# A decode step of attention plus a gated MLP on one core: whole wo loads, w_out on 128 lanes, another order of the last tiles, and part of wq's last rows on 2, 4 and 8 transfer engines

## The chip, the core and the metric

The kernel runs on one core of a Trainium2 chip. The core has TensorE (PE, matrix products, with its weight loads listed apart as PEld), VectorE (DVE), ScalarE (ACT), GpSimd (POOL) and SyncE (SP), which here issues nearly all transfers. Sixteen transfer engines (numbered 0 to 15 below) move data from the chip's memory (HBM) to the on-chip memory of 128 partitions, also called lanes. PE writes its results to an accumulator memory of its own (PSUM). The engines run on their own queues and wait for one another through semaphores.

The metric is the device time of one execution in microseconds (us): the median of several runs.

## The reference

Four sequences (B = 4), one new token each, model width D = 640. Both branches read the layer-normalised x.

- Attention: q = xn @ wq gives 32 heads of 128. Each of the 128 pairs of sequence and head has its own cache of 4096 keys and 4096 values of 128. The scores are q.k / sqrt(128); softmax over 4096; the weighted sum of the values; then all heads @ wo (4096 x 640).
- Gated MLP: z = gelu(xn @ w_in), 1728 wide, cut into z1 and z2 (Fh = 864 each); z2 is layer-normalised, multiplied by the scalar w_sp and shifted by b_sp (the sequence length is one); z1 times this @ w_out (864 x 640).

```python
xn = _layernorm(x, axis=-1)
return x + _A_ref(xn, k_cache, v_cache, wq, wo) + _B_ref(xn, w_in, w_sp, b_sp, w_out)
```

All data is bf16. The caches are 2 x 134 MB; the other inputs together are below 14 MB.

## The kernel before

**Tiles.** The caches are cut into NT = 32 tiles each of keys and of values: tile i holds 4 heads (HT) of one sequence. A tile is 128 partitions x 16384 elements, 4 MB, and one load (L118) brings it; partition p has 128 positions (NC) of one head. Tiles of four sequences form a group; there are HG = 8 groups.

**Slots.** Key and value tiles, the two parts of wq, and w_in with w_out share five slots (`KV_SLOTS`). A load can be issued when what was in its slot before has been used. The list `loads` (L123) is the order in which tiles are loaded: k0, k1, then v and k in turn, then k30, k31 and the last four values. `load_to(n)` issues loads up to the n-th of this list and is called at fixed places of the main loop. The last value tile comes in four pieces (`V_CUTS`).

**Per key tile**, in four quarters: `product` (DVE, L370) multiplies keys by the query, `fold_half` (DVE, L382) adds the two halves of each key, `sums` (PE, L394) adds further with an identity as weights, `row_sums` (DVE, L405) finishes the scores. `lane_max`, `turn_max`, `head_max`, `spread_max` and `exps` make the softmax weights of a tile during the next one. `weighted` (PE, L462) multiplies a value tile by its weights, 128 small matmuls. After four tiles of a group `group_den`, `group_norm` and `group_proj` divide and multiply by that group's wo rows (L492).

**Order.** The instructions of PE, DVE, ACT and SP stand in each queue as the program writes them (`manual_schedule`, L509). In the main loop tile i's keys are used, and the values of tile `lag`: i - 1 up to 28, none at 29, i - 2 after that. Tile 30's values come after the loop, between the softmax steps of tile 31, and then tile 31's in four cuts.

**Loads of weights.** SP issues, in this order: wq's first four rows of each partition (L90, 4 MB), its fifth rows (1 MB, 8 KB in each partition), w_in (L101), w_out (L102), k0, k1. wq, x and w_in are laid out so that partition p holds rows 5p to 5p + 4; the normalised x is turned to the same layout by five transposes (L197). w_out lies on 96 partitions of nine rows (FP = 96, NFC = 9), so w_in's columns are read with a step of nine (L248) and the MLP's hidden values are on 96 partitions. wo comes by group (`load_wo`, L137), one load of 128 partitions x 4 x 640 in one buffer; group 5's alone is cut into loads of 8, 4, 2, 1, 1 and 112 partitions (`WO_PROBE`), and the last group's into four, by head.

**The DMA semaphores.** Loads take eight semaphores in turn; a load whose semaphore still belongs to an earlier one is issued only after that one has landed. A load is divided over several transfer engines, and each of these adds one event to its semaphore.

Of the kernel before, what the change touches and what calls it, by code (L numbers as in the profile page):

```python
# [13 lines left out]
AX = mybir.AxisListType  # L14

KV_SLOTS = 5
PROBED = 5
WO_PROBE = (0, 8, 12, 14, 15, 16, 128)


@with_exitstack
def kernel(
# [34 lines left out]
    HD2 = Dh // 2  # L57
    RW = 8
    SLOT = NC * Dh
    FP = 96  # L60
    NFC = Fh // FP
    NOH = D // 2
    assert NFC * FP == Fh
# [14 lines left out]
    def slot(name):  # L78
        return kv.tile([P, SLOT], BF16, tag="kv", name=name)
# [5 lines left out]

    wq_v = A_wq.rearrange("(p c) n -> p c n", c=DC)
    wq_parts = []
    for c0, c1 in ((0, HT), (HT, DC)):
        t = slot("wq")[:, 0 : (c1 - c0) * HD].rearrange("p (c n) -> p c n", n=HD)
        nc.sync.dma_start(out=t, in_=wq_v[:, c0:c1, :])  # L90
        wq_parts += [(t, i) for i in range(c1 - c0)]

    wsp_bf = const.tile([1, 1], BF16)
    bsp_bf = const.tile([1, 1], BF16)
# [2 lines left out]

    w_sb = slot("w_sb")
    w_in_sb = w_sb[:, 0 : DC * F].rearrange("p (c n) -> p c n", c=DC)
    w_out_sb = w_sb[0:FP, DC * F : DC * F + NFC * D].rearrange("p (k n) -> p k n", k=NFC)  # L100
    nc.sync.dma_start(out=w_in_sb, in_=B_w_in.rearrange("(p c) n -> p c n", c=DC))  # L101
    nc.sync.dma_start(out=w_out_sb, in_=B_w_out.rearrange("(p k) n -> p k n", k=NFC))  # L102

    def kv_view(cache, i):
        hg, b = divmod(i, Bsz)
# [15 lines left out]
        tiles[i] = t[:].rearrange("p (c d) -> p c d", d=Dh)  # L121

    loads = [("k", 0), ("k", 1)]  # L123
    for i in range(NT - 4):
        loads += [("v", i), ("k", i + 2)]
    loads += [("k", NT - 2), ("k", NT - 1)] + [("v", i) for i in range(NT - 4, NT)]
    n_loaded = [0]

    def load_to(n):
        while n_loaded[0] < min(n, len(loads)):  # L130
            load(*loads[n_loaded[0]])
            n_loaded[0] += 1

# [3 lines left out]
    def load_wo(j):  # L137
        wo_tiles[j] = wop.tile([P, HT, D], BF16, name="wo")
        if j == HG - 1:
            for hh in range(HT):  # L140
                nc.sync.dma_start(out=wo_tiles[j][:, hh, :], in_=wo_v[j][:, hh, :])
            return
        cuts = WO_PROBE if j == PROBED else (0, P)
        for p0, p1 in zip(cuts, cuts[1:]):
            nc.sync.dma_start(out=wo_tiles[j][p0:p1], in_=wo_v[j][p0:p1])

    load_to(2)

# [43 lines left out]
    )  # L192

    xn_v = xn_bf[:].rearrange("b (p c) -> b c p", c=DC)
    xnT_ps = ps_m.tile([P, DC, Bsz], BF16, tag="m")
    for c in range(DC):
        nc.tensor.transpose(  # L197
            out=xnT_ps[:, c, :], in_=xn_v[:, c, :], identity=ident[:Bsz, :Bsz]
        )
    xnT = const.tile([P, DC, Bsz], BF16)  # L200
# [34 lines left out]

    gm = {}
    for name in ("zz", "gw", "gt", "gz"):
        gm[name] = work.tile([FP, 2, NFC, Bsz], FP32, name=name)
    gm["sq"] = work.tile([FP, NFC, Bsz], FP32, name="sq")
    gm["st"] = work.tile([1, 5 * Bsz], FP32, name="st")  # L240
    gm["ac"] = work.tile([1, 2 * Bsz], FP32, name="ac")
    gm["yT"] = work.tile([FP, NFC, Bsz], BF16, name="yT")

    def gmlp():
        zz, gw, gt, gz, sq = (gm[n] for n in ("zz", "gw", "gt", "gz", "sq"))
        zT = ps_pv.tile([FP, 2, NFC, Bsz], FP32, tag="pv", name="zT")
        for t in range(2):
            w_t = w_in_sb[:, :, t * Fh : (t + 1) * Fh].rearrange("p c (f k) -> p c k f", k=NFC)  # L248
# [25 lines left out]
        for src, at in ((gz[:, 1, :, :], 0), (sq[:], Bsz)):  # L274
            for k in range(NFC):
                nc.tensor.matmul(  # L276
                    out=s_ps[:, at : at + Bsz],
                    lhsT=ones_sq[:FP, 0:1],
                    rhs=src[:, k, :],
                    start=(k == 0),  # L280
                    stop=(k == NFC - 1),
                )
# [41 lines left out]
        nc.vector.tensor_tensor(  # L324
            out=sq[:],
            in0=gz[:, 1, :, :],
            in1=ac_sb[:FP, None, 0:Bsz].to_broadcast([FP, NFC, Bsz]),
            op=ALU.mult,
        )
        nc.vector.tensor_tensor(  # L330
            out=sq[:],
            in0=sq[:],
            in1=ac_sb[:FP, None, Bsz : 2 * Bsz].to_broadcast([FP, NFC, Bsz]),
            op=ALU.add,
        )
        nc.vector.tensor_tensor(out=gm["yT"][:], in0=gz[:, 0, :, :], in1=sq[:], op=ALU.mult)
        for k in range(NFC):
            for half in range(2):
                nc.tensor.matmul(
                    out=out_sum(half),  # L340
                    lhsT=gm["yT"][:, k, :],
                    rhs=w_out_sb[:, k, half * NOH : (half + 1) * NOH],
                    start=False,
                    stop=False,
                )
# [56 lines left out]
    def row_sums(i, half):  # L402
        if half == 0:
            scores[i] = small.tile([P, NC], FP32, name="s_sb")
        nc.vector.tensor_reduce(  # L405
            out=scores[i][:, half * HC : (half + 1) * HC],
            in_=sums_ps.pop((i, half))[:],
            axis=AX.X,
            op=ALU.add,
        )  # L410

    def lane_max(i):
        m1 = small.tile([P, 1], FP32, name="m1")
        nc.vector.tensor_reduce(out=m1[:], in_=scores[i][:], axis=AX.X, op=ALU.max)  # L414
        maxes[i] = m1
# [84 lines left out]
    def group(i, fn):  # L500
        if 0 <= i < NT and i % Bsz == Bsz - 1:
            fn(i // Bsz)

    def at(i, fn, *args):
        if 0 <= i < NT:
            fn(i, *args)

    E = mybir.EngineType
    with tc.manual_schedule(engines={E.PE, E.DVE, E.Activation, E.SP}):  # L509
        stage_q(0)  # L510
        stage_q(1)
        gmlp()
        load_to(3)
        for i in range(NT):
            lag = i - 1 if i < NT - 3 else None if i == NT - 3 else i - 2
# [5 lines left out]
            if i < NT - 1:  # L521
                group(i - 2, group_proj)
# [81 lines left out]
```

## Time and profile before

| | |
|---|---|
| time, median of 3 runs | 681.03 us (680.99 to 681.11) |
| the profiled execution's own time | 680.97 us |
| its span | 679.2 us |
| PE, DVE, ACT busy | 406.8, 506.7, 94.3 us |
| bytes from HBM | 282.24 MB, 416 GB/s over the span |
| products L370 | 128 x 2286 ns |
| folds L382 | 128 x 1219 ns |
| zT matmuls L251 | 90, 15.6 us together |
| waits of DVE's products for key tiles | 81.9 us |

The page cuts the span into 40 slices; its rows are busy tenths, and under DMA the mean share of the 16 transfer engines with the GB/s that they moved. The chain of waits goes back from the last instruction to what released it, again and again. The transfer view can be asked for one stretch of time: packets, MB, and the share of 16 engines that the packets' durations make up. The trace also holds each packet (size, start, duration) and each semaphore event of a load; it does not name the engine of a packet, but packets of one engine follow each other without a gap, so an engine can be followed.

### The profile page before, as it was taken

Reading aid. Unit: us, or ns where it says so; the run is one execution under the profiler, and the core shown is the slowest. Engines: PE = TensorE matmul, PEld = TensorE weight load, DVE = VectorE, ACT = ScalarE, POOL = GpSimd, SP = SyncE. Lnnn points to the kernel's source line nnn. Section 1 sums busy time; section 2 is a strip of 40 time slices with the busy share of each in tenths; the row PEclk is TensorE's granted clock in tenths of the full one; section 3 lists DMA queues with packets and bytes.
Section 4 is the critical chain, followed back from the end, with each engine's and each line's share of the span. In section 5 each row is a group of like instructions: output and inputs, shape, how many; then the busy total and the mean of one; then the engine's idle time right before and its main releaser. Section 6 shows DMA issues by size and latency. Waiting matters only on the chain.

```text
span 679.2 us, 11555 instructions
## 1 busy us (share of the span) xinstructions
PE 406.8 (60%) x5225; PEld 227.8 (34%) x5225; DVE 506.7 (75%) x432; ACT 94.3 (14%) x329; POOL 2.7 (0%) x12
## 2 busy tenths in 40 slices
PE   1945777556656556665555665555664456655677
PEld 1931334323332233333223333223333133331345
DVE  1069999877779777688776778687766877779991
ACT  0111211101111100111110111110111101111111
POOL 1000000000000000000000000000000000000000
PEclk9999675567656656656566756555665667656665
DMA  9999999999999999999999999999999999999994
GB/s 374 375 432 432 427 431 422 427 432 430 421 432 428 431 430 423 429 431 432 429 422 429 431 429 426 427 428 431 429 349 405 429 430 429 424 428 431 430 419 168
DMA packets 14563, 282.99 MB, mean 417 GB/s; under 512 B 1350, under 2 KB 5458, under 8 KB 5714
## 3 DMA queue, kind: packets, MB, share of 16 engines
q1 hardware_dynamic: 14494, 282.25, 98.3%
q8 instruction: 41, 0.67, 0.4%
q14 instruction: 8, 0.07, 0.0%
q10 hardware_dynamic: 20, 0.01, 0.0%
HBM read 282.24 MB, written 0.01 MB: 416 GB/s over the span
## 4 chain that ended last, share of the span: by engine, by line
DMA 63%; DVE 18%; PE 17%; issue 1%; ACT 0%; SPq 0%; DVEq 0%
DMA k_nat<-in_A_k_cache_dram 55%; DVE prod L370 10%; PE s_ps L394 8%; DMA v_nat<-in_A_v_cache_dram 5%; PE pv L462 5%; DVE folded L382 5%; DMA w_sb<-in_B_w_in_dram 3%; PE zT L251 2%; DVE s_sb L405 2%; DVE m L414 1%; ACT pm L447 0%; DVE nm L424 0%; PE qbc_ps L356 0%; PE out_ps L492 0%; PE ln_ps L276 0%
## 5 line engine op out<-in xcount | busy, mean ns | idle before, releaser
L370 DVE TENSOR_TENSOR prod<-k_nat,qbc 128x4096 bf16<-128x4096 bf16 x128 | 292.6, 2286 | 83.5 <-DMA k_nat<-in_A_k_cache_dram 81.9
L394 PE MATMUL s_ps<-folded,ident 128*128 128x512 bf16 x512 | 225.6, 621 | 74.5 <-DVE folded L382 74.5
L382 DVE TENSOR_TENSOR folded<-prod 128x2048 bf16<-128x2048 bf16 x128 | 156.1, 1219 | 3.3
L394 PEld LDWEIGHTS <-ident 128*128 128x128 bf16 x512 | 71.9, 141 | 182.9 <-issue 182.0
L462 PE MATMUL pv<-pm,v_nat 128*128 128x4 bf16 x4096 | 111.7, 167 | 2.2 <-DMA v_nat<-in_A_v_cache_dram 1.8
L462 PEld LDWEIGHTS <-v_nat 128*128 128x128 bf16 x4096 | 109.3, 100 | 7.4 <-DMA v_nat<-in_A_v_cache_dram 2.9
L419 PE MATMUL mT<-ident_f,m 128*1 128x128 f32 x32 | 11.2, 351 | 114.4 <-DVE m L414 114.4
L447 ACT ACTIVATE pm<-s_sb,nb 32x128 bf16<-32x128 f32 x128 | 73.9, 577 | 2.6
L443 ACT COPY nb<-nb_ps 128x4 f32<-128x4 f32 x32 | 5.2, 162 | 477.9 <-PE nb_ps L435 477.9
L435 PE MATMUL nb_ps<-nm,scale_row 1*128 1x4 f32 x64 | 18.0, 349 | 57.9 <-DVE nm L424 57.9
L419 PEld LDWEIGHTS mT<-ident_f,m 128*1 128x1 f32 x32 | 2.5, 79 | 140.9 <-DVE m L414 112.1
L405 DVE TENSOR_REDUCE s_sb<-s_ps 128x64 f32<-128x512 f32 x64 | 43.6, 681 | 7.3 <-PE s_ps L394 4.3
L435 PEld LDWEIGHTS nb_ps<-nm,scale_row 1*128 1x128 f32 x64 | 15.9, 305 | 67.5 <-issue 56.7
L447 ACT ACTIVATION_READ_ACCUMULATOR pm<-s_sb,nb 32x1 f32 x128 | 32.1, 251 | 0.0
L478 DVE RECIPROCAL rden<-den 128x16 f32<-128x16 f32 x8 | 2.1, 258 | 34.6 <-PE den L474 34.6
L364 ACT CAST qbc<-qbc_ps 128x128 bf16<-128x128 f32 x32 | 8.4, 266 | 75.8 <-PE qbc_ps L356 75.8
L251 PE MATMUL zT<-xnT,w_sb 128*96 128x4 bf16 x90 | 15.6, 312 | 0.5 <-DMA w_sb<-in_B_w_in_dram 0.5
L251 PEld LDWEIGHTS <-w_sb 128*96 128x96 bf16 x90 | 15.6, 267 | 0.7 <-DMA w_sb<-in_B_w_in_dram 0.7
L258 DVE COPY zz<-zT 96x72 f32<-96x72 f32 x1 | 0.2, 229 | 16.6 <-PE zT L251 16.6
L356 PEld LDWEIGHTS <-qT 128*32 128x32 bf16 x128 | 3.4, 99 | 24.1 <-issue 23.6
L215 DVE CAST qT<-q_ps 128x128 bf16<-128x128 f32 x1 | 0.3, 292 | 14.6 <-PE q_ps L207 14.6
L207 PE MATMUL q_ps<-xnT,wq 128*128 128x4 bf16 x160 | 4.6, 166 | 9.8 <-DMA wq<-in_A_wq_dram 9.8
(67 smaller groups left out, 75.7 us busy)
## 6 DMA issues: line engine op xcount, KB each, us to landing
k_nat<-in_A_k_cache_dram SPq DMA_DIRECT2D x32, 4096.0 KB, 42.3
v_nat<-in_A_v_cache_dram SPq DMA_DIRECT2D x31, 4096.0 KB, 35.2
wq<-in_A_wq_dram SPq DMA_DIRECT2D x1, 4096.0 KB, 12.2
wo<-in_A_wo_dram SPq DMA_DIRECT2D x6, 640.0 KB, 44.7
w_sb<-in_B_w_in_dram SPq DMA_DIRECT2D x1, 2160.0 KB
v_nat<-in_A_v_cache_dram SPq DMA_DIRECT2D x1, 2048.0 KB
w_sb<-in_B_w_out_dram SPq DMA_DIRECT2D x1, 1080.0 KB
wq<-in_A_wq_dram SPq DMA_DIRECT2D x1, 1024.0 KB
```

Source lines behind the costliest of these rows:

```text
L251: nc.tensor.matmul(out=zT[:, t, k, :], lhsT=w_t[:, c, k, :], rhs=xnT[:, c, :], start=(c == 0), stop=(c == DC - 1),)
L364: nc.scalar.copy(out=qbcs[i][:], in_=qb_ps[:])
L370: nc.vector.tensor_tensor(out=t[:], in0=k_tiles[i][:, q * QC : (q + 1) * QC, :], in1=qbcs[i][:, None, :].to_broadcast([P, QC, Dh]), op=ALU ...
L382: nc.vector.tensor_tensor(out=folds[i, half][:, part * QC : (part + 1) * QC, :], in0=t[:, :, 0:HD2], in1=t[:, :, HD2:Dh], op=ALU.add,)
L394: nc.tensor.matmul(out=s[:], lhsT=ident[:], rhs=t[:, :, g * RW : (g + 1) * RW], start=(g == 0), stop=(g == n - 1),)
L405: nc.vector.tensor_reduce(out=scores[i][:, half * HC : (half + 1) * HC], in_=sums_ps.pop((i, half))[:], axis=AX.X, op=ALU.add,)
L414: nc.vector.tensor_reduce(out=m1[:], in_=scores[i][:], axis=AX.X, op=ALU.max)
L419: nc.tensor.transpose(out=mT[:], in_=maxes[i][:], identity=ident_f[:])
L435: nc.tensor.matmul(out=nb_ps[:], lhsT=scale_row[:], rhs=maxes[i][:], start=True, stop=True)
L443: nc.scalar.copy(out=nb[:], in_=maxes.pop(i)[:])
L447: nc.scalar.activation(out=pm[ps, :, hh], in_=s_sb[ps, :], func=ACT.Exp, bias=nb[ps, hh : hh + 1], scale=scale_qk, accum_out=a[ps, hh, b : ...
L462: nc.tensor.matmul(out=pvs[hg][:, :, b], lhsT=v_nat[:, c, :], rhs=pm[:, c, :], start=(c == 0), stop=(c == NC - 1),)
```

## The change

- `load_wo`: group 5's wo comes in one load, as the other groups' do.
- w_out lies on 128 partitions of six rows (NFF = 6), and the 96 rows that are left over come in a second load as a seventh part (FT = 96). w_in's columns are read with a step of six, the last 96 of each half directly. The MLP's tiles have 128 partitions and seven parts; `zz` is cleared first, and copied from PSUM in two pieces.
- The load order is built in one loop, with a second key tile after v23 and after v27 (`EXTRA_K`), so keys 26 to 29 stand one value tile earlier than before; `turns` gives the value tile of each step from it: i - 1 up to 24, none at 25, i - 2 from 26 to 29, none at 30, and 28 at 31. Values 29 and 30 come after the loop, after tile 31's softmax. `pump` issues every load whose slot's last use stands in the program, in place of the counts given to `load_to`.
- wq's fifth rows come in four loads of 1024 columns (2 KB in each partition). The first is laid out as before. In the three others the rows are grouped with a slowest dimension of 2, 4 and 8: partition p then holds another row, and three more transposed copies of the normalised x (`xn_l`) carry that order. The query matmuls of heads 8 to 31 take the copy of their group.

```diff
-PROBED = 5
-WO_PROBE = (0, 8, 12, 14, 15, 16, 128)
+EXTRA_K = (24, 28)
...
-    FP = 96
-    NFC = Fh // FP
+    NFF = Fh // P
+    NFC = NFF + 1
+    FT = Fh - NFF * P
...
-    for c0, c1 in ((0, HT), (HT, DC)):
-        t = slot("wq")[:, 0 : (c1 - c0) * HD].rearrange("p (c n) -> p c n", n=HD)
-        nc.sync.dma_start(out=t, in_=wq_v[:, c0:c1, :])
-        wq_parts += [(t, i) for i in range(c1 - c0)]
+    t = slot("wq")[:, 0 : HT * HD].rearrange("p (c n) -> p c n", n=HD)
+    nc.sync.dma_start(out=t, in_=wq_v[:, 0:HT, :])
+    wq_parts += [(t, i) for i in range(HT)]
+    assert DC == HT + 1
+    SPREADS = (2, 4, 8)
+    NW = HD // (len(SPREADS) + 1)
+    t = slot("wq")[:, 0:HD]
+    nc.sync.dma_start(out=t[:, 0:NW], in_=wq_v[:, HT, 0:NW])
+    for g, k in enumerate(SPREADS, 1):
+        nc.sync.dma_start(
+            out=t[:, g * NW : (g + 1) * NW],
+            in_=wq_v[:, HT, g * NW : (g + 1) * NW].rearrange("(b a) n -> a b n", a=k),
+        )
+    wq_parts.append((t.rearrange("p (c n) -> p c n", c=1), 0))
...
-    w_out_sb = w_sb[0:FP, DC * F : DC * F + NFC * D].rearrange("p (k n) -> p k n", k=NFC)
+    w_out_sb = w_sb[:, DC * F : DC * F + NFC * D].rearrange("p (k n) -> p k n", k=NFC)
     nc.sync.dma_start(out=w_in_sb, in_=B_w_in.rearrange("(p c) n -> p c n", c=DC))
-    nc.sync.dma_start(out=w_out_sb, in_=B_w_out.rearrange("(p k) n -> p k n", k=NFC))
+    nc.sync.dma_start(
+        out=w_out_sb[:, 0:NFF, :], in_=B_w_out[0 : NFF * P].rearrange("(p k) n -> p k n", k=NFF)
+    )
+    nc.sync.dma_start(out=w_out_sb[:FT, NFF, :], in_=B_w_out[NFF * P : Fh])
...
-    for i in range(NT - 4):
-        loads += [("v", i), ("k", i + 2)]
-    loads += [("k", NT - 2), ("k", NT - 1)] + [("v", i) for i in range(NT - 4, NT)]
+    n_k = 2
+    for i in range(NT):
+        loads.append(("v", i))
+        for _ in range(2 if i + 1 in EXTRA_K else 1):
+            if n_k < NT:
+                loads.append(("k", n_k))
+                n_k += 1
+    occupants = [("w", 0), ("w", 1), ("w", 2)] + loads
+    used = set()
     n_loaded = [0]
 
-    def load_to(n):
-        while n_loaded[0] < min(n, len(loads)):
+    def pump():
+        while n_loaded[0] < len(loads):
+            at = n_loaded[0] + 3 - KV_SLOTS
+            if at >= 0 and occupants[at] not in used:
+                return
             load(*loads[n_loaded[0]])
             n_loaded[0] += 1
...
-        cuts = WO_PROBE if j == PROBED else (0, P)
-        for p0, p1 in zip(cuts, cuts[1:]):
-            nc.sync.dma_start(out=wo_tiles[j][p0:p1], in_=wo_v[j][p0:p1])
-
-    load_to(2)
+        nc.sync.dma_start(out=wo_tiles[j][:], in_=wo_v[j])
+
+    pump()
...
-    xnT_ps = ps_m.tile([P, DC, Bsz], BF16, tag="m")
+    NX = DC + len(SPREADS)
+    xnT_ps = ps_m.tile([P, NX, Bsz], BF16, tag="m")
+    for g, k in enumerate(SPREADS):
+        xn_l = work.tile([Bsz, P], BF16, name=f"xn_l{g}")
+        nc.vector.tensor_copy(
+            out=xn_l[:].rearrange("b (a q) -> b a q", a=k),
+            in_=xn_v[:, HT, :].rearrange("b (q a) -> b a q", a=k),
+        )
...
-                rhs=xnT[:, c, :],
+                rhs=xnT[:, c if c < HT or h * Dh < NW else DC + h * Dh // NW - 1, :],
...
+            f1 = t * Fh + NFF * P
+            w_t = w_in_sb[:, :, t * Fh : f1].rearrange("p c (f k) -> p c k f", k=NFF)
             for k in range(NFC):
                 for c in range(DC):
                     nc.tensor.matmul(
-                        out=zT[:, t, k, :],
-                        lhsT=w_t[:, c, k, :],
+                        out=zT[: P if k < NFF else FT, t, k, :],
+                        lhsT=w_t[:, c, k, :] if k < NFF else w_in_sb[:, c, f1 : f1 + FT],
                         rhs=xnT[:, c, :],
                         start=(c == 0),
                         stop=(c == DC - 1),
                     )
-        nc.vector.tensor_copy(out=zz[:], in_=zT[:])
+        nc.vector.tensor_copy(out=zz[:, :, 0:NFF, :], in_=zT[:, :, 0:NFF, :])
+        nc.vector.tensor_copy(out=zz[:FT, :, NFF, :], in_=zT[:FT, :, NFF, :])
...
+    turns = {}
+    lag = 1
+    for i in range(NT):
+        if any(("k", i) == x and ("k", i + 1) == y for x, y in zip(loads, loads[1:])) and i:
+            lag += 1
+        elif i >= lag:
+            turns[i] = i - lag
...
-            if lag is not None:
-                at(lag, weighted)
-                group(lag, group_den)
+            if j is not None:
+                weighted(j)
+                group(j, group_den)
+                used.add(("v", j))
             row_sums(i, 0)
             product(i, 3)
             fold_half(i, 3)
-            if lag is not None:
-                group(lag, group_norm)
+            if j is not None:
+                group(j, group_norm)
             sums(i, 1)
-            if i == 0:
-                load_to(4)
-            else:
-                load_to(4 + 2 * i)
+            used.add(("k", i))
+            pump()
             if i % Bsz == 2 and i // Bsz < HG - 1:
                 load_wo(i // Bsz)
-        load_to(len(loads))
         load_wo(HG - 1)
-        i = NT - 1
-        row_sums(i, 1)
-        lane_max(i)
-        weighted(i - 1, 0, 32)
-        turn_max(i)
-        head_max(i)
-        weighted(i - 1, 32, 48)
-        spread_max(i)
-        exps(i)
-        weighted(i - 1, 48, NC)
+        row_sums(NT - 1, 1)
+        lane_max(NT - 1)
+        turn_max(NT - 1)
+        head_max(NT - 1)
+        spread_max(NT - 1)
+        exps(NT - 1)
+        for j in range(turns[NT - 1] + 1, NT - 1):
+            weighted(j)
         for c0, c1 in zip(V_CUTS, V_CUTS[1:]):
-            weighted(i, c0, c1)
+            weighted(NT - 1, c0, c1)
             if c0 == 0:
                 group_den(HG - 1)
         group_norm(HG - 1)
```

More of the change, by code (lines that the diff above doesn't have):

```diff
@@ L59 @@
     SLOT = NC * Dh
-    FP = 96
-    NFC = Fh // FP
+    NFF = Fh // P
+    NFC = NFF + 1
+    FT = Fh - NFF * P
     NOH = D // 2
-    assert NFC * FP == Fh
     const = ctx.enter_context(tc.tile_pool(name="const", bufs=1))
@@ L194 @@
     xn_v = xn_bf[:].rearrange("b (p c) -> b c p", c=DC)
-    xnT_ps = ps_m.tile([P, DC, Bsz], BF16, tag="m")
+    NX = DC + len(SPREADS)
[6 more added lines that the diff above has]
+        )
+        nc.tensor.transpose(
+            out=xnT_ps[:, DC + g, :], in_=xn_l[:], identity=ident[:Bsz, :Bsz]
+        )
     for c in range(DC):
@@ L199 @@
         )
-    xnT = const.tile([P, DC, Bsz], BF16)
+    xnT = const.tile([P, NX, Bsz], BF16)
     nc.vector.tensor_copy(out=xnT[:], in_=xnT_ps[:])
@@ L237 @@
     for name in ("zz", "gw", "gt", "gz"):
-        gm[name] = work.tile([FP, 2, NFC, Bsz], FP32, name=name)
-    gm["sq"] = work.tile([FP, NFC, Bsz], FP32, name="sq")
+        gm[name] = work.tile([P, 2, NFC, Bsz], FP32, name=name)
+    nc.gpsimd.memset(gm["zz"][:], 0.0)
+    gm["sq"] = work.tile([P, NFC, Bsz], FP32, name="sq")
     gm["st"] = work.tile([1, 5 * Bsz], FP32, name="st")
     gm["ac"] = work.tile([1, 2 * Bsz], FP32, name="ac")
-    gm["yT"] = work.tile([FP, NFC, Bsz], BF16, name="yT")
+    gm["yT"] = work.tile([P, NFC, Bsz], BF16, name="yT")
     def gmlp():
         zz, gw, gt, gz, sq = (gm[n] for n in ("zz", "gw", "gt", "gz", "sq"))
-        zT = ps_pv.tile([FP, 2, NFC, Bsz], FP32, tag="pv", name="zT")
+        zT = ps_pv.tile([P, 2, NFC, Bsz], FP32, tag="pv", name="zT")
         for t in range(2):
-            w_t = w_in_sb[:, :, t * Fh : (t + 1) * Fh].rearrange("p c (f k) -> p c k f", k=NFC)
+            f1 = t * Fh + NFF * P
+            w_t = w_in_sb[:, :, t * Fh : f1].rearrange("p c (f k) -> p c k f", k=NFF)
             for k in range(NFC):
@@ L277, in gmlp @@
                     out=s_ps[:, at : at + Bsz],
-                    lhsT=ones_sq[:FP, 0:1],
+                    lhsT=ones_sq[:, 0:1],
                     rhs=src[:, k, :],
@@ L326, in gmlp @@
             in0=gz[:, 1, :, :],
-            in1=ac_sb[:FP, None, 0:Bsz].to_broadcast([FP, NFC, Bsz]),
+            in1=ac_sb[:, None, 0:Bsz].to_broadcast([P, NFC, Bsz]),
             op=ALU.mult,
@@ L332, in gmlp @@
             in0=sq[:],
-            in1=ac_sb[:FP, None, Bsz : 2 * Bsz].to_broadcast([FP, NFC, Bsz]),
+            in1=ac_sb[:, None, Bsz : 2 * Bsz].to_broadcast([P, NFC, Bsz]),
             op=ALU.add,
@@ L337, in gmlp @@
         for k in range(NFC):
+            w = P if k < NFF else FT
             for half in range(2):
@@ L340, in gmlp @@
                     out=out_sum(half),
-                    lhsT=gm["yT"][:, k, :],
-                    rhs=w_out_sb[:, k, half * NOH : (half + 1) * NOH],
+                    lhsT=gm["yT"][:w, k, :],
+                    rhs=w_out_sb[:w, k, half * NOH : (half + 1) * NOH],
                     start=False,
@@ L512 @@
         gmlp()
-        load_to(3)
+        used.update(occupants[:3])
+        pump()
         for i in range(NT):
-            lag = i - 1 if i < NT - 3 else None if i == NT - 3 else i - 2
+            j = turns.get(i)
             product(i, 0)
@@ L520 @@
             at(i - 1, turn_max)
-            if i < NT - 1:
-                group(i - 2, group_proj)
+            group(turns.get(i - 1, -1), group_proj)
             product(i, 1)
@@ L538 @@
             fold_half(i, 3)
-            if lag is not None:
-                group(lag, group_norm)
+            if j is not None:
+                group(j, group_norm)
             sums(i, 1)
-            if i == 0:
-                load_to(4)
-            else:
-                load_to(4 + 2 * i)
+            used.add(("k", i))
+            pump()
             if i % Bsz == 2 and i // Bsz < HG - 1:
                 load_wo(i // Bsz)
-        load_to(len(loads))
         load_wo(HG - 1)
-        i = NT - 1
-        row_sums(i, 1)
-        lane_max(i)
-        weighted(i - 1, 0, 32)
-        turn_max(i)
-        head_max(i)
-        weighted(i - 1, 32, 48)
-        spread_max(i)
-        exps(i)
-        weighted(i - 1, 48, NC)
+        row_sums(NT - 1, 1)
[6 more added lines that the diff above has]
+            weighted(j)
         for c0, c1 in zip(V_CUTS, V_CUTS[1:]):
-            weighted(i, c0, c1)
+            weighted(NT - 1, c0, c1)
             if c0 == 0:
```

## The prediction

> **What bounds the kernel now.** I read the slices of the page first, then the chain of waits, then SP's own waits, and last the transfer view cut into short windows.
>
> The page's slices (40 of 17 us each, and the chain under them):
>
> ```profile
> DMA  9999999999999999999999999999999999999994
> GB/s 374 375 432 432 427 431 422 427 432 430 421 432 428 431 430 423 429 431 432 429 422 429 431 429 426 427 428 431 429 349 405 429 430 429 424 428 431 430 419 168
> DMA 63%; DVE 18%; PE 17%; issue 1%; ACT 0%; SPq 0%; DVEq 0%
> ```
>
> The transfer engines never pause. 282 MB at about 430 GB/s is the time; there are three dents, at the start (374), in slices 29 and 30 (349, 405), and in the last one. VectorE is busy 75% and waits for keys. The dents, in the transfer view, one window each: the last rows of wq, then w_in, then w_out, then the wo load in six pieces:
>
> ```profile
> q1 hardware_dynamic: 79, 0.65, 101.7%
> ...
> q1 hardware_dynamic: 96, 1.66, 101.7%
> ...
> q1 hardware_dynamic: 44, 0.51, 92.9%
> ...
> DMA packets 539, 3.02 MB, mean 282 GB/s; under 512 B 35, under 2 KB 463, under 8 KB 463
> ```
>
> Share times 16 engines times window over packets is one packet's time. 12.7 to 14.2 us: 79 packets of 8192 B, 309 ns. 15.2 to 19: 96 of 17280 B, 644 ns; both are 27 GB/s per engine. 20.9 to 23.2: w_out, 44 of 11520 B, 777 ns, where the same rate would be 432. The engines are as busy, but move half. 500.8 to 511.5, the six pieces of wo: 282 GB/s. What w_out (96 lanes) and the 112-lane piece share is that an engine's lanes are not those it writes in a 128-lane load. The packet records say the same singly: a 1280 B packet takes 53 ns alone and 86 to 114 on average in each us from 501 to 510; a 32 KB packet beside it 1.5 to 2.0 us in place of 1.21.
>
> The end, from the chain of waits after 600 us and SP's waits there:
>
> ```profile
> 642.53 3.58 PE pv L462 x128
> 646.11 3.45 PE s_ps L394 x8
> ...
> 670.77 1.85 PE pv L462 x64
> 672.62 0.45 PE den L474 x2
> 673.07 1.70 PE pv L462 x64
> ...
> 675.02 1.27 PE out_ps L492 x8
> ...
> SPq L118 <- DVE prod L370: 33.4, 3, 15.6
> SPq L141 <- DMA v_nat<-in_A_v_cache_dram: 13.9, 2, 9.4
> ```
>
> The last landing (fourth wo piece) is at 673.49 by the semaphore events, yet the end still runs through keys of tile 31: arithmetic ends last, by a little.
>
> One more reading carries the forecast. Every load ends with one semaphore event per transfer engine. For tile v29 they spread from 643.4 to 651.7: lags of 0.0 to 0.8 us on six engines, 3.7 and 4.4 on two, 5.9 to 8.3 on eight. The lags grow in steps of 1.55 us where a 16 KB instruction fetch (41 in the trace) stands between an engine's packets. I followed each engine's packets through the pieces of 8, 4, 2 and 1 rows: the engines that carried all of them (numbers 0 and 1) have 0.7 and 3.7, numbers 2 and 3 have 0.8 and 4.4, the late eight are two of 4 to 7 and six of 8 to 15. Loads divide evenly, so the latest engine sets every landing.
>
> **The change part by part**, as the shift of one engine's end.
>
> Whole wo load of group 5. The lead engine's v22 to v23 takes 25.2 us; v18 to v19, with a whole load between, 21.2. Gain 3.9 on engines 8 to 15, 4.6 and 5.0 on 0 and 1, which had more pieces. SP's lane waits there (468 to 510) go too; they starved nobody.
>
> w_out on 128 lanes. From w_in's end to k0's end the lead engine took 14.6 (19.60 to 34.22). Now 9.71 for k0, 8 packets of 7680 B at 290 ns (between 4096 B, 159, and 8192 B, 309), and a 96-lane rest of 6 packets at 53 to 110: 12.5. Gain 2.1 for all; 1.0 if the rest disturbs k0 as before, 2.4 if not at all.
>
> wq's last rows. Before, 8 packets of 309 ns on each engine: 2.47. After, on engines 8 to 15, 8 of 2 KB, 82 ns each (between 1280 B, 53, and 4096 B, 159): 0.66, gain 1.8; at worst 0, since as many bytes still go to their lanes. On engines 0 and 1, 8 + 64 + 32 + 16 = 120 packets. Alone they are 9.8: +7.4. But 112 of them go to lanes that another engine is filling with w_in. The rows of shared lanes: w_out 777 against 432 (1.8 times), 1280 B at 86 to 114 against 53 (1.6 to 2.2). I take 2.0: the neighbour streams all the time, and engines 2 to 7 come through the same lanes. 0.66 + 112 x 0.164 = 19.0: +16.6. Ends: 1.0 (+7.4) and, three at one place for half of them, 2.5 (+21.1).
>
> [...]
>
> Start. Eight DMA semaphores go round; five wq loads and three small ones take them all, so w_out's issue now waits for wq's first part (landed 12.9, issued 2.2 before), with the rest, k0 and k1 queued behind it on SP. Engines 8 to 15 have w_in until 18.1, so 5 us cover it. Queries wait for the last group: 31.8 instead of 15; v0 and k2 are issued near 33, not 20, and engines run dry only at 41. w_in lands near 37 instead of 21; 60 strided matmuls of 174 ns and the small chain (6.3) put the first product at about 54, not 43.0. Then v2 goes out near 85 where lead engines would take it at 81: they idle 4 us, and are not the last. Three copies and transposes more (0.2 us each) end before 12.9: nothing. zT falls from 90 to 70 matmuls, ln_ps from 36 to 28: beside transfers.
>
> Order of the last tiles. Keys 26 to 29 come one tile (9.7 us) earlier; product 31 then ends near 660, so arithmetic no longer ends last. Three value tiles are left for PE at the end, 3.5 us each, the first two under v31's 9.7. From the fourth wo piece's landing to the end it then takes 0.3 (last matmuls) and what follows 676.3 (2.9): 3.2, where now it is 5.7 (673.49 to 679.2). Gain 2.5; at worst 0.
>
> **Sum**, against the profiled execution, 680.97 (span 679.2, 1.8 around it; 0.06 under the median): the engine of lag 3.7 gets 16.6 - 5.0 - 2.1 = +9.5, so 13.2 where the latest had 8.3: +4.9. With -2.5 at the end: 683.4. The late eight end at 8.3 - 6.0 + 4 of idling = 6.3 and don't matter.
>
> **Rivals.**
> Balance (faster): the loaded engines write at their lone rate. Lag 3.7 + 7.4 - 7.1 = 4.0, -4.3 against 8.3, with the end 674.2. For it: engines 0 to 3 do have room. Against it: every shared window above. It decides below 143 ns per 2 KB packet (1.74 times): there the wq term is +14.2, which the gains cancel, and the time is 681.0.
> Worse sharing: 2.5 times, lag 17.7, 687.9; w_out's slowness on all engines alike speaks for it, few engines crossing speaks against it.
> No grouping at all: the loads go to 16 engines, and the late eight set the end: 8.3 - 3.9 - 2.1 + 0.2 = 2.5, 672.7. The nested pieces speak against it.
>
> **How the numbers follow.** About 0.2% is what this kernel's measurement can tell (1.4 us). Sharing near 2 times: 0.50, of which a tenth ends within 0.2% of before; worse sharing 0.15; balance 0.27, its upper part within 0.2%; no grouping 0.08. Faster 0.31, same 0.12, slower 0.57. Range from balance, 674, to 689, a little above the worse sharing; the likeliest case's own is 680.5 to 686.5.
>
> **What would show it.** Right: p1's two semaphore events (of the load on 2 engines) 10 us or more after those of the first quarter; w_in landing after 33; first product after 49; no dent in slices 29 and 30; two engines last in every later landing; the fourth wo piece 3 us before the end. Wrong: w_in landing before 30 and the late eight still last, or 2 KB packets under 143 ns.

## The result and the profile after

The changed kernel takes 682.34 us (median; 681.73 to 683.99) against 680.8 (680.0 to 681.2) for the kernel before: a ratio of 1.0026, interval 1.0018 to 1.0033. It is slower by about 1.5 us. Its profiled execution took 682.4 us, with a span of 680.6 (before 680.97 and 679.2).

The page first: the transfer row, the GB/s of the 40 slices, and the chain under them.

```profile
DMA  8999999999999999999999999999999999999993
GB/s 312 340 429 433 427 429 428 419 431 431 429 430 425 428 430 431 421 432 432 429 430 423 429 429 430 427 427 430 429 432 424 428 430 427 428 432 430 433 409 130
...
DMA 55%; DVE 25%; PE 16%; SPq 2%; issue 1%; DVEq 0%
```

The dent in slices 29 and 30 is gone (349 and 405 before, now 429 and 432). The first two slices are lower (374 and 375 before, now 312 and 340), the last one too (168, now 130), and SP's queue has come into the chain with 2%. SP's instructions at the start (start, duration, line, how many):

```profile
1.65 11.20 SPq L96 DMA_DIRECT2D wq<-in_A_wq_dram  x3
12.89 1.30 SPq L110 DMA_DIRECT2D w_sb<-in_B_w_in_dram  x1
...
15.62 1.76 SPq L130 DMA_DIRECT2D k_nat<-in_A_k_cache_dram  x2
```

Issuing the three grouped loads held SP for 11.2 us (0.69, 8.09 and 2.33 us singly; the two loads ahead of them took 0.41 each). w_in was issued at 12.89, where it had been 1.63. Next, stretches of the start: the time, its length, the busy time and count of PE, PEld, DVE, ACT and POOL, the clock, the share of the transfer engines, and GB/s. The kernel before, and then the changed one with a fourth stretch around the wo load of group 5:

```profile
12.40:14.20 1.80, 0.27 (x4) 0.18 (x4) 0.00 (x0) 0.00 (x0) 0.00 (x0) 1.00 1.02 432
14.20:23.00 8.80, 6.71 (x176) 6.36 (x176) 0.29 (x1) 1.72 (x3) 0.00 (x0) 1.00 1.04 372
23.00:30.00 7.00, 7.00 (x43) 7.00 (x42) 0.00 (x0) 0.00 (x0) 0.00 (x0) 1.00 1.06 393
```

```profile
12.40:14.20 1.80, 0.67 (x19) 0.59 (x20) 0.00 (x0) 0.00 (x0) 0.00 (x0) 1.00 0.46 157
14.20:23.00 8.80, 2.05 (x71) 1.88 (x68) 0.00 (x0) 0.00 (x0) 0.00 (x0) 1.00 0.97 276
23.00:30.00 7.00, 2.76 (x84) 2.32 (x84) 0.29 (x1) 0.24 (x2) 0.00 (x0) 1.00 1.11 352
500.00:512.00 12.00, 10.63 (x150) 6.03 (x150) 8.69 (x6) 2.74 (x10) 0.00 (x0) 0.64 1.01 433
```

Two losses show in the changed kernel's first two lines. From 12.4 to 14.2 the engines are half idle (share 0.46): most have run out of loads. From 14.2 to 23 they are busy (0.97) and move 276 GB/s: the packets themselves take longer. The last line is the whole wo load, without a dent (before, the six pieces had 287 GB/s in the same stretch).

Landings, by the semaphore events, from the first transfer engine to the last: k0 at 37.67 to 45.51 (34.60 to 36.66 in run 9 below, whose start is that of before); the fourth wo piece at 664.32 to 673.86 (before 665.30 to 673.49). So the last landing is 0.4 us later, and the end stands 6.74 us behind it, where it was 5.7. The sum is the 1.4 us of the span. The chain after that landing:

```profile
661.73 3.69 PE pv L495 x135
665.42 2.17 issue
667.59 3.55 PE pv L495 x128
671.14 1.27 issue
672.41 1.66 PE pv L495 x57
674.08 0.45 PE den L507 x2
674.52 1.70 PE pv L495 x64
...
676.48 1.27 PE out_ps L525 x8
```

PE ends last: 384 matmuls of three value tiles in a row, with two stops of 2.17 and 1.27 us in which it waits for nothing that the profile shows.

### The profile page after: what moved, and what is told of

The parts are those of the page before. It is cut to its first block, busy times and chain, and to the rows that moved or that the text cites. A ratio compares the mean times of both kernels' runs of the same rounds, so it can differ in the third digit from the quotient of the medians.

```text
span 680.6 us, 11504 instructions
## 1 busy us (share of the span) xinstructions
PE 394.1 (58%) x5196; PEld 214.0 (31%) x5196; DVE 507.6 (75%) x436; ACT 94.3 (14%) x329; POOL 2.8 (0%) x13
## 4 chain that ended last, share of the span: by engine, by line
DMA 55%; DVE 25%; PE 16%; SPq 2%; issue 1%; DVEq 0%
DMA k_nat<-in_A_k_cache_dram 55%; DVE prod L403 14%; PE s_ps L427 9%; DVE folded L415 7%; PE pv L495 6%; DVE s_sb L438 3%; SPq L96 2%; DVE m L447 1%; DVE nm L457 0%; PE qbc_ps L389 0%; PE den L507 0%; SPq L110 0%; PE out_ps L525 0%; DVE rden L511 0%; SPq L114 0%
## 5 line engine op out<-in xcount | busy, mean ns | idle before, releaser
L236 PEld LDWEIGHTS <-wq 128*128 128x128 bf16 x160 | 4.7, 104 | 18.7 <-DMA wq<-in_A_wq_dram 18.7
L447 DVE TENSOR_REDUCE m<-s_sb 128x1 f32<-128x128 f32 x32 | 9.2, 286 | 1.1
L457 DVE TENSOR_REDUCE nm<-mT 1x4 f32<-1x128 f32 x32 | 8.7, 272 | 0.6 <-PE mT L452 0.6
```

The lines of the kernel that those rows point to most:

```text
L236: nc.tensor.matmul(out=q_ps[:, h, :], lhsT=t[:, i, h * Dh : (h + 1) * Dh], rhs=xnT[:, c if c < HT or h * Dh < NW else DC + h * Dh // NW - ...
L457: nc.vector.tensor_reduce(out=nm[:], in_=maxes[i][:].rearrange("a (h p) -> a h p", h=HT), axis=AX.X, op=ALU.max, negate=True,)
```

## Experiments

The kernel before, measured beside each group of runs, had medians of 680.76 to 681.0. "Last landing" is the latest event of the fourth wo piece; 673.49 before, 673.86 changed.

**1. The change without the groups.**

```diff
-    SPREADS = (2, 4, 8)
+    SPREADS = ()
```

> The changed kernel with wq's fifth rows in one plain load on 16 engines (as before the change), all else as changed. Theory A (the groups cost every engine, at the start): lead engines' k1 lands near 41.8 instead of 47.4, the last wo piece near 667.5 (673.5 before the change, less 3.9 for the whole wo load, less 2.1 for w_out) instead of 673.9, and the end stays 6.7 behind it: 675 to 676.5 us. Rival B (the groups even out the engines and pay for themselves): the late eight engines come last again, the last piece at 673.9 or later, 682 or more.

Measured: 676.79 us, ratio 0.994 (0.9927 to 0.9952). The last landing is at 667.43. The same stretches of the start:

```profile
12.40:14.20 1.80, 0.27 (x4) 0.18 (x4) 0.00 (x0) 0.00 (x0) 0.00 (x0) 1.00 1.00 423
14.20:23.00 8.80, 6.79 (x205) 6.44 (x206) 0.29 (x1) 1.72 (x3) 0.00 (x0) 1.00 1.10 449
23.00:30.00 7.00, 2.91 (x63) 2.73 (x61) 2.83 (x17) 1.83 (x3) 0.00 (x0) 1.00 0.92 388
```

Both losses are gone, and so is w_out's dent of the kernel before. Whole wo and w_out together move the last landing by 673.49 - 667.43 = 6.06 us; the prediction's two terms make 6.0. The groups cost 673.86 - 667.43 = 6.4 us of landing and 5.5 us of time. The end stands 7.4 us behind the landing, again with PE last and two stops (2.28 and 2.64 us), so a part of the gain is not cashed.

**2. The groups alone.** The kernel before, with nothing changed but wq's last rows in four loads, three of them grouped (and the three turned copies of x).

> The kernel before, with the grouped loads of wq's fifth rows as the only change. Theory A: the lead engines lose some 5.6 us by k1, engines 0 and 1 some 11; the last landing goes from 673.5 to 679 or 680, and the time from 681 to 685.5 to 687.5 us. Rival B: no slower than before, 679 to 681.

Measured: 691.5 us, 1.0154 (1.014 to 1.0168): +10.5 us, more than either expected. Here w_out still lies on 96 lanes, and in the stretch in which it runs beside the groups less is moved than in any other run:

```profile
23.00:30.00 7.00, 1.46 (x49) 1.29 (x46) 0.00 (x0) 0.00 (x0) 0.00 (x0) 1.00 1.10 208
```

w_out's packets took 899 ns in mean (737 in the kernel before), w_in's 1022 (946 in the changed kernel). Two loads that each put engines onto lanes of others (that they do is argued, as said below run 7) seem to cost more together than the sum of their prices: 10.5 us here, where the groups beside a w_out on 128 lanes cost 5.5 (run 1); the order of the tiles and the wo pieces differ from the changed kernel too, so the run doesn't give the size of it.

**3. The order of before.** The changed kernel with the list of loads, the turns and the end of the loop as they were.

```diff
-        for _ in range(2 if i + 1 in EXTRA_K else 1):
+        for _ in range(3 if i == NT - 5 else 1):
```

> The changed kernel with the load order, the turns of the values and the end of the loop as before the change. If the new order is worth what was forecast (arithmetic no longer ends last): 2.5 us slower, 684.8. If the end is now held by the three value tiles left to PE (its matmuls run without a pause but for two stops from 661.7 to 676.2, and the last landing plus 3.2 would be 677.1): the old end, 5.7 behind the last landing in place of 6.7, gives 681.3, 1 us faster.

Measured: 681.82 us, 1.0012 (1.0003 to 1.0021). The new order gains nothing beside the groups; if anything it is 0.5 us the dearer. With the old order the last landing is at 674.69 and the end 5.0 behind it: tile 31's softmax ends late, but PE has only 128 matmuls left, and no stop among them.

**4. The tail woven.** The changed kernel, with the products of value tile 29 placed between the softmax steps of tile 31, where PE waits for other engines.

```diff
+        weighted(NT - 3, 0, 32)
         row_sums(NT - 1, 1)
         lane_max(NT - 1)
         turn_max(NT - 1)
         head_max(NT - 1)
+        weighted(NT - 3, 32, 48)
         spread_max(NT - 1)
         exps(NT - 1)
-        for j in range(turns[NT - 1] + 1, NT - 1):
-            weighted(j)
+        weighted(NT - 3, 48, NC)
+        weighted(NT - 2)
```

> The changed kernel with tile 29's values taken between the softmax steps of tile 31 in place of after them; loads and order of loads unchanged. If PE's 384 matmuls after the softmax hold the end: some 3 us less, end set by the last landing (673.9 + 3.2 = 677.1), 678.5 to 679.5 us. If the two stops of PE (2.2 and 1.3 us, each behind an instruction fetch) are what matters, they stay, and the gain is 0 to 1: 681.3 to 682.3.

Measured: 679.47 us, 0.9978 (0.9968 to 0.9987): 2.9 us below the changed kernel, though its last landing is no earlier (674.34). The chain:

```profile
667.79 0.35 PE pv L495 x7
668.14 1.18 issue
669.31 1.66 PE pv L495 x57
...
671.42 1.26 PE pv L495 x48
...
672.70 0.60 PE pv L495 x16
```

The end is now 3.36 us behind the last landing, so moving those 128 matmuls is enough to free it. It is not their place alone: the stops went from 2.17 + 1.27 us to one of 1.18 with it, and the run doesn't separate the two.

**5. Four loads, none grouped.** The same four column loads of 2 KB per partition, all in the old layout.

```diff
-    SPREADS = (2, 4, 8)
+    SPREADS = ()
...
-    nc.sync.dma_start(out=t[:, 0:NW], in_=wq_v[:, HT, 0:NW])
-    for g, k in enumerate(SPREADS, 1):
...
+    for n0 in range(0, HD, HD // 4):
+        nc.sync.dma_start(out=t[:, n0 : n0 + HD // 4], in_=wq_v[:, HT, n0 : n0 + HD // 4])
```

> The changed kernel with the same four column loads of wq's last rows, all plain on 16 engines: the same 2 KB packets, the same number of loads and semaphore turns, the rows left where they were. If the cost of the grouping lies in spreading packets over few engines (held issue, shared lanes): the time of the run without groups, 676.8, within 1 us: 676 to 678; the last wo piece near 667.5, w_in landed by 21.5 us, no window under 350 GB/s before 30 us, each issue under 1 us. If it lies in 2 KB packets or in the extra loads taking semaphores: 680.5 to 683, with w_out, k0 and k1 issued late as in the changed kernel.

Measured: 677.43 us, 0.9946 (0.9932 to 0.996); last landing 667.85. w_in landed from 20.41 to 21.99, w_out was issued at 13.0 because it has to wait for a semaphore's turn (in the trace of the changed kernel its issue waits for the semaphore of wq's first load, whose events run from 12.41 to 13.08), and both cost nearly nothing (0.6 us against run 1). SP:

```profile
1.20 2.10 SPq L95 DMA_DIRECT2D wq<-in_A_wq_dram  x4
3.34 0.47 SPq L111 DMA_DIRECT2D w_sb<-in_B_w_in_dram  x1
13.00 0.33 SPq L112 DMA_DIRECT2D w_sb<-in_B_w_out_dram  x1
```

Four issues take 2.10 us where three grouped ones took 11.20. Short packets, more loads and the semaphores' turns are not the cause; the grouping is.

**6. The groups in reverse, 8, 4, 2.**

```diff
-    SPREADS = (2, 4, 8)
+    SPREADS = (8, 4, 2)
```

> The changed kernel with the groups in the reverse order: 8 engines first, then 4, then 2. The engines carry exactly the same packets. If an issue is held because engines 0 and 1 have some 80 to 110 packets before them, the first two issues are short (under 1 us), the third or what follows it is held, and w_in is still issued near 12 us; the time then stays within 1 us of the changed kernel: 681.3 to 683.3. If each grouped load has a price of its own kind (the 4-engine load was the one held 8.09 us), that load is held again, now in second place, and the 8-engine one in front is short. If the order of the sharing sets the cost (the load on 2 engines beside the others), the time moves by over 1 us either way.

Measured: 682.02 us, 1.0017 (1.0008 to 1.0026), the same as the changed kernel. SP:

```profile
1.64 2.45 SPq L96 DMA_DIRECT2D wq<-in_A_wq_dram  x3
4.13 9.93 SPq L110 DMA_DIRECT2D w_sb<-in_B_w_in_dram  x1
```

Now all three grouped issues pass (1.28, 0.55, 0.53 us), and the load after them, a plain one on 16 engines, is held 9.93 us. So the hold is no property of a grouped load. By the order of the issues it goes with the packets that engines 0 and 1 still have before them. Counting 8 for each load on 16 engines, an issue passed with 16 (the changed kernel's load on 2 engines) and with 8 + 8 + 16 + 32 = 64 (the same load here), and was held with 8 + 8 + 64 = 80 (the changed kernel's load on 4) and with 128 (w_in here).

**7. w_in and w_out ahead of the groups.** The grouped loads are issued after both.

```diff
+    nc.sync.dma_start(out=w_out_sb[:FT, NFF, :], in_=B_w_out[NFF * P : Fh])
+    for g, k in enumerate(SPREADS, 1):
+        nc.sync.dma_start(
+            out=t_q[:, g * NW : (g + 1) * NW],
...
```

> The changed kernel with w_in and w_out issued before the three grouped loads; k0 and what follows stay behind them. The engines then have 3 MB to move while SP is held, so the stop at 12.4 to 14.2 us goes. If the held issue is what costs: 677 to 679.5, with w_in landed by 22. If the shared lanes cost (w_in's packets near 1000 ns in place of 644, whoever waits): the sharing moves to k0 or stays with w_in, and the time is 680.5 to 682.5; the queries come later, so v0 and k2 are issued after 31 us and the time may reach 684.

Measured: 682.01 us, 1.0019 (1.0009 to 1.0028). w_in landed undisturbed (18.30 to 18.95), and its packets took 644 ns. The price moved to what followed, k0 and k1:

```profile
14.20:23.00 8.80, 0.79 (x30) 0.71 (x27) 0.00 (x0) 0.00 (x0) 0.00 (x0) 1.00 0.97 364
23.00:30.00 7.00, 0.00 (x0) 0.00 (x0) 0.00 (x0) 0.00 (x0) 0.00 (x0) 1.00 0.87 243
```

A 32 KB packet, 1214 ns alone, took 1567 in mean from 12 to 40 us (1.5 to 2.7 us while the groups ran). The idle stretch moved too (a share of 0.87 from 23 to 30), so this run does not take the hold away; it puts other loads beside the groups, and the time stays.

**Where the 5.8 us go.** Taking the mean over the sixteen engines of when each has landed its part of k0, the changed kernel stands at 39.20, run 1 at 33.41: 5.8 us, or 93 us of engine time. At the last landing the same difference is 669.55 - 663.65 = 5.9: all of it is lost before k0 and kept to the end. I summed, from 11.5 to 40 us, what every packet took beyond its lone time (2 KB 82 ns, w_in's 17280 B 644, w_out's 7680 B 291, 1280 B 55, 32 KB 1214):

| us of engine time beyond lone | run 1 | changed | run 6 | run 7 |
|---|---|---|---|---|
| 2 KB packets | - | 13.9 | 11.7 | 18.7 |
| w_in | 0.0 | 38.7 | 44.3 | 0.0 |
| w_out, both loads | 1.6 | 16.7 | 13.5 | 1.1 |
| key tiles | 6.9 | 10.0 | 7.0 | 54.7 |
| all | 8.6 | 79.3 | 76.5 | 74.4 |

So 71 of the 93 us are longer packets, four fifths of them those of loads that were not grouped; the idle stretch, 1.8 us at a share of 0.46, is 1.0 us on each engine, another 16. The three grouped versions lose nearly the same, wherever the loss falls. That the lanes are the cause is argued, from what these loads share with the 96-lane w_out and the 112-lane wo piece (16 events each, so, evenly divided, 6 and 7 lanes to an engine in place of 8): no record names the lanes of a packet, and no run keeps a load on few engines and each engine on its own lanes. The grouped loads also read wq's rows in another order.

**8. No groups and the tail woven:** runs 1 and 4 together.

> The changed kernel without the groups and with the weighted products of value tile 29 placed between the softmax steps of tile 31. If the two costs stand side by side: last wo piece near 667.5, the end 3.3 us behind it, 1.8 around the span: 672 to 673.8. If without the groups keys or the chip's arithmetic set the end, it stays near the 676.8 of the run without groups: 675.5 to 677.

Measured: 672.52 us (672.48 to 672.78), 0.9878 (0.9864 to 0.9892), 8.3 us below the kernel before and faster than both. Its slices and its end:

```profile
GB/s 371 420 438 431 429 425 431 425 429 431 430 417 434 431 429 435 415 435 437 422 433 427 422 430 435 433 415 437 428 434 421 429 427 429 435 418 433 432 421 223
```

```profile
660.88 0.43 PE pv L495 x10
661.30 1.54 issue
662.84 1.58 PE pv L495 x54
...
666.82 1.27 PE out_ps L525 x8
```

The last landing is at 667.48, the span ends at 670.7: 3.2 us, which is the end that the prediction had given to the changed kernel itself. The two costs stand side by side: 5.5 us of groups, and 4.3 of the tail (676.79 - 672.52), more than the 2.9 of run 4: there the landing was 0.5 us later than in the changed kernel, and run 1's two stops, which the weaving shortens, are longer (4.92 us against 3.44).

**9. The whole wo load alone.**

```diff
-WO_PROBE = (0, 8, 12, 14, 15, 16, 128)
+WO_PROBE = (0, 128)
```

> The kernel before with the wo load of group 5 in one piece, and nothing else. The prediction's term is 3.9 us off the engines that end last: last wo piece at 673.5 - 3.9 = 669.6. Its end then goes by arithmetic or by the landing plus 5.7: 676.9 to 678.5. If the six pieces' price was hidden or is paid elsewhere: 680.5 to 681.5.

Measured: 676.67 us, 0.994 (0.9927 to 0.9952); last landing 669.20, 4.3 us earlier (predicted 3.9). The stretch of the pieces, at 287 GB/s before:

```profile
500.00:512.00 12.00, 6.46 (x116) 3.67 (x112) 8.29 (x7) 0.00 (x0) 0.00 (x0) 0.77 1.03 428
```

**10. w_out on 128 lanes alone** (run 3 without the groups and with the six pieces of wo, so all else but `pump` is of before).

> The changed kernel without the groups, with the order of loads of before and with the six pieces of wo: w_out on 128 lanes alone. The prediction's term is 2.1 us off every engine: last wo piece at 671.4, 678.5 to 679.5. If half the 96-lane price stays: 1.0 us, 680. If arithmetic holds the end: 680.5 to 681.5 with an earlier landing.

Measured: 678.68 us, 0.9962 (0.995 to 0.9974); last landing 671.51, 2.0 us earlier (predicted 2.1). In time, runs 9 and 10 gain 4.1 and 2.1; added, they would make 674.6 with the old order, and run 1, which has both with the new order, took 676.79. By this sum, which no run shows directly, the new order costs some 2 us once the landing is early.

**11. Half of the rows on 8 engines**, in the fastest version: one plain load of 2048 columns and one grouped, 128 packets of 4 KB.

```diff
-    SPREADS = ()
+    SPREADS = (8,)
```

> The fastest version so far (672.5) with half of wq's last rows in one grouped load on 8 engines, 128 packets of 4 KB. In the changed kernel the groups cost all engines 4.7 us in mean, 75 us of engine time, for 384 packets and 786 KB. Priced by bytes: 512 KB cost 49 us, 3.1 us on each engine, less 1.2 us that engines 8 to 15 no longer carry: 674.3. Priced by packets: 1.6 less 1.2: 672.9. If evening pays and the price came from the concentration on two engines alone: 671.3. Issues of SP should all be short, with at most 24 packets on an engine.

Measured: 677.61 us, 0.9956 (0.9944 to 0.9969): 5.1 us slower than run 8, more than any of the three expected. No issue was held (0.78 us for the grouped load) and the engines did not run dry. The packets alone did it:

```profile
14.20:23.00 8.80, 4.48 (x156) 4.31 (x156) 0.18 (x1) 0.00 (x0) 0.00 (x0) 1.00 0.99 266
```

Busy to 0.99, and 266 GB/s. From 14 to 18 us a 4 KB packet took 366 to 380 ns against 159 alone, and w_in's took 1473 against 644: 2.3 times both (over all packets 330 and 905 ns, 2.1 and 1.4 times). In mean over the engines k0 lands 36.99 - 33.44 = 3.55 us later, 57 us of engine time. By bytes, the changed kernel's 93 us for 384 packets of 2048 B would give 62 for these 128 of 4096 B, and by packets 31; without the idling, which run 11 doesn't have, the 71 us would give 47 and 24. So bytes come nearer than packets, in the one pair of runs that there is. My forecast of 674.3 by bytes failed on where it falls: the first engines to land lost 2.3 us, and those that carried the group 2.5 more; the last landing moved by 4.8 (667.48 to 672.31). There the two latest engines have lags of 9.3 and 9.6 us, where in run 8 none is over 8.1: engines that are late anyway seem to be among the eight that carry the group.

## Why the prediction was right, and where it was not

The direction and the size came out (683.4 forecast, 682.34 measured), but by luck: two large errors cancelled. With the end as forecast the change would have been faster, as run 4 shows (679.47, with 681.0 for the kernel before beside it). As a ledger of the span, each term of the prediction beside what the runs showed:

| term | forecast, us | shown |
|---|---|---|
| whole wo load, late engines | -3.9 | -4.3 (run 9) |
| w_out on 128 lanes | -2.1 | -2.0 (run 10) |
| wq's rows on 2, 4, 8 engines | by engine: +16.6 on 0 and 1, -1.8 on 8 to 15 | last landing +6.4, first +4.9, mean +5.9 (against run 1) |
| last landing, all three | +4.9 | +0.4 |
| order of the last tiles, end behind it | -2.5 (5.7 to 3.2) | +1.0 (5.7 to 6.74) |
| sum | +2.4 | +1.4 |

- **The two gains** are right in place and size, and they add: 4.3 and 2.0 alone, 6.06 together. Reading a lone packet's time off one window, and an engine's loss off the spread of the semaphore events, was enough.
- **wq's last rows, on engines 0 and 1.** The term's 120 packets need loads that go to 2, 4 and 8 engines, numbers 0 and 1 among them each time. No run from before the change shows that of a grouped load of 128 rows: there it was only pieces of wo, of 8, 4 and 2 rows, that ended with 8, 4 and 2 events. In the changed kernel the three loads end with 2, 4 and 8 events (and have a single early one each, at 2.72, 10.90 and 13.27), and two engines alone come far behind at k0, with lags of 7.2 and 7.8 us. Nor does a run show that their packets cross to lanes of others; the factor for it was the author's estimate. The step that failed is "I take 2.0". The grouped 2 KB packets took 118 ns in mean (512 of 2 KB at 109, less the 128 plain ones at 82), 1.4 times the lone time and not 2.0. By k0 the latest engine has lost 45.51 - 34.85 = 10.7 us against run 1, not 16.6. At 118 ns the prediction's own break-even (143 ns) says faster (by its sum 678.2); its condition for being wrong was met, and it was right only through two things that it did not see, the price on the late engines and the end.
- **wq's last rows, on the late engines.** The step that failed is "at worst 0, since as many bytes still go to their lanes", and with it the late eight that "don't matter". The first engine to land k0 lost 37.67 - 32.95 = 4.7 us. The engines that stream pay most: w_in's packets went from 644 to 946 ns in mean (38.7 us in all), while the grouped 2 KB packets went from 82 to 118 (13.9 us). The prediction put the price of a shared lane on the newcomer alone. The trace of before had the sign of it: beside the 112-lane wo piece, 32 KB packets took 1.5 to 2.0 us in place of 1.21, and I quoted it without giving the streamers a term. These runs show the slowing, not what brings it about. The 4 us of idling that the prediction gave to these engines did not come either: the first landings from k0 to v2 follow each other at 9.7 us.
- **The wait on SP.** The prediction had w_out wait for a semaphore with 5 us of cover. What came was another wait: SP held 8.09 us in one issue, w_in itself issued at 12.89, and 1.0 us of idling on each engine. It did not see this, and run 5 shows that the foreseen turn costs next to nothing (0.6 us in all against run 1).
- **Start.** w_in "near 37" landed from 23.60 to 33.05, the first product "at about 54" came at 45.54, because engines 0 and 1 were faster than taken. The two events of the load on 2 engines came at 20.98 and 21.16, some 7 to 8 us after those of the first quarter, where the prediction asked for 10 or more. "Two engines last in every later landing" holds for k0 and k1 (lags of 7.2 and 7.8 us, 14 engines within 3.0) and fades later: at the end one has 9.5 and ten have 5.9 to 7.9.
- **Order of the last tiles.** Product 31 did end near 660 (s_ps at 659.16), and the whole 2.5 was lost after it. The step that failed is "3.5 us each, the first two under v31's 9.7": the matmuls take that while they run, but the stops of PE have no term. Values 29 to 31 stand after tile 31's softmax in PE's queue, so their 384 matmuls begin only at 661.73 and have little slack; the busy pieces of the chain (3.69, 3.55, 1.66, 0.45, 1.70) would end at 672.8, ahead of the last landing at 673.86, but PE stops for 3.4 us among them and ends at 676.2. Run 4 moves 128 of them forward, keeps one stop of 1.18, and finds nearly the forecast end (3.36, and 3.2 in run 8). So the term holds for an order with slack for the stops, which the code did not have.

The rivals: "no grouping", with 672.7, is what run 8 measures once the tail is woven (672.52). "Balance" needed under 143 ns a packet, got it, and did not come, since it too left the streamers at their lone rate. "Worse sharing" (2.5 times on engines 0 and 1) did not occur in the changed kernel; run 11 comes nearest, with 2.1 on its eight engines.

Two readings of the prediction are slightly off, and nothing hangs on them: the semaphore events of v29 run from 643.97 to 652.19, some 0.5 us later than it says, with nearly the same lags; and its chances for slower add up to 0.60 by its own split, not 0.57.

What stays open: why PE stops. In the changed kernel and in runs 1, 4 and 8 each stop begins within 1.4 us of the start of a 16 KB instruction fetch of about 1.0 to 1.1 us (in the changed kernel at 665.04 and 669.86, with stops from 665.42 and 671.14). One thing more speaks for the fetches: counted in PE's own instructions in the trace (matmuls, weight loads, and at the first stop of the changed kernel 45 semaphore instructions and a drain), the stops of all these runs stand after 9921 or 10177 of them, 256 apart. Runs 3, 6 and 7 stop once more, for 0.9 to 1.7 us near 92 us, after 1217, which is 34 times 256 before 9921, and again just after a fetch. Run 1 has three transposes fewer at the start (six instructions), and its first stop comes three matmuls later in the values (138 in place of 135), at the same count. Nothing was run that removes a fetch, and the records don't say for which engine it is.

## To carry to other kernels

Where transfers bound a kernel, price a load by what it does to the others too: here engines that, as argued above, wrote into lanes which others were filling slowed those by more than they lost themselves (384 packets of 2 KB cost 93 us of engine time; of the 71 that are longer packets, four fifths fell on other loads). Evening out the engines by moving work between them must be measured as the mean over all engines' landings, not only the last one. And when loads come earlier, look at where the dependent instructions stand in their engine's queue: work that could fill another wait gains nothing if it is written behind it (tile 29's products, moved ahead in run 4, took 2.9 us off).

## What was unexpected of the hardware

- **Issues were held while a few engines had many packets before them.** Behind the load of 64 packets on each of two engines the next issue took 8.09 us and the one after 2.33 (5.04 and 2.25 in run 7); with the groups in reverse the plain load behind them took 9.93; in run 11, with 16 packets on each of eight engines, none was held. Counted when the issue begins, these runs passed one with 64 packets on an engine and held one with 80. When a hold ends doesn't follow from one count: at 10.47 in the changed kernel some 74 were left on engines 0 and 1, at 14.06 in run 6 some 100.
- **Grouped loads and the loads beside them slowed each other** (that they cross lanes is argued), 1.4 times for the grouped packets and 1.5 for w_in's in the changed kernel (in mean); with one group on eight engines (run 11) 2.1 and 1.4 times, and 2.3 for both from 14 to 18 us, where the changed kernel's w_in is at 1.7. Beside a w_out on 96 lanes (run 2) the grouping cost 10.5 us, beside one on 128 lanes 5.5.
- **PE stopped for 0.6 to 2.6 us** within the last rows of small matmuls, in each version with the new order, each time within 1.8 us of an instruction fetch and after 9921 or 10177 of its own instructions.
